# Attention scores as fp32 products on halves of TensorE's rows, with an eight-block weight ring and block products from the fifth chunk on

## The chip, the cores and the metric

The kernel runs on one core of one Trainium2 chip. The metric is the time of the whole kernel in device microseconds; the profiles give the span of one execution and what each engine did in it.

## The reference

Four batches of eight heads, 768 positions, 64 values a head. Each position sees the first `n_sink` = 4 keys and the last `window` = 128; its output goes through a feed-forward block with 512 inputs and 2048 inner values.

```python
scores = scale * np.matmul(q, k.transpose(0, 1, 3, 2))
...
keep = is_sink | in_window
scores = np.where(keep, scores, -1000000000.0)
scores = scores - np.max(scores, axis=-1, keepdims=True)
a = np.exp(scores)
a = a / (np.sum(a, axis=-1, keepdims=True) + 1e-09)
return np.matmul(a, v).astype(np.float32)
...
h = x @ w_in
g = h - np.tanh(h)
return (g @ w_out).astype(np.float32)
```

## The kernel before

**Chunks and units.** The 3072 rows are cut into 12 chunks of 256 rows (two query tiles of 128), numbered `cc` = 0 to 11: the first chunk of batches 0 to 2, then the other two of each of these, then the three of batch 3. A chunk's attention is four units `u`, each a pair of heads. Keys are laid out so that a query tile's keys (four sink keys and 256 positions) are 260 columns in a row; in the first tile of a batch only the last 132 of them are read by what follows.

**Attention of a unit** (`scores`, `normalise`, `turn`, `attend`). For each query tile and each head a product of queries and keys goes to a bank of its own in PSUM; VectorE merges and masks (`merge`), ScalarE takes the exponent, sums are inverted, TensorE transposes (L599), VectorE, ScalarE and GpSimd mask the transposed blocks, and TensorE multiplies with the values (L662). There the two heads of a pair have 64 output rows each and use the lower and upper 64 columns of the array.

**Two ways of scores.** For the first 12 units (`raw(u)`) queries and keys are multiplied as they are, in fp32 (L507). The 64 rows of the other head are zeros in the queries (cleared by GpSimd, L353, loaded in halves by `_load_pair`), so each product uses all 128 rows. The profile records such an fp32 product as two passes. For the later 36 units `split` makes high and low parts: ScalarE rounds keys and queries (L473, L483), VectorE subtracts (L478, L486), and four products of one pass each (L514) make the scores of a tile of two heads.

**Feed-forward.** A step `n` is one chunk with one of eight groups `g` of inner values. Its first half (`mm1`, L793) is 24 products of 256 columns. Its second half is 12 products of 512 columns (`mm2`, L863) or, from chunk `SA` = 5 on, 21 products of 256 columns that make the same result by blocks (`mm7`, L897). The block products need three sums of weight blocks for each group, the edge blocks: `derive` copies and adds them by DMA (L992, L995) and splits them. From chunk 3 on the first half's weights come from memory through a ring of seven blocks (`stream`; tiles `ring` and `spare`).

**Order.** Everything is added to a list with an engine, a price and a due time; `Work.order` puts it in order with these prices, and the engines run it in that order. The prices and due times are the constants `FIRST`, `PACE`, `LEAD` and others. Loads of the later units go through GpSimd's queue, the others through SyncE's.

Of the kernel before, what the change touches and what calls it, by code (L numbers as in the profile page):

```python
# [18 lines left out]
P = 128  # L19
# [21 lines left out]
def kernel(  # L41
# [20 lines left out]
    for m in range(2):  # L62
        first = pts[:, m].rearrange("p h a b -> p (h a b)")
        early.append((first[:, :KW], first[:, KW : KW + 2 * CH].rearrange("p (h s) -> p h s", h=2)))
    et = mybir.EngineType
    with tc.manual_schedule(engines={et.PE, et.SP, et.DVE, et.Activation, et.Pool}):
# [3 lines left out]
        for m in range(2):  # L70
            k, q = early[m]
            nc.sync.dma_start(k, kp[0, m, :, :KW])
            _load_pair(nc, q, qd[0, 2 * m : 2 * m + 2, :, :CH], True)
# [23 lines left out]
def _load_pair(nc, q, src, zeros):  # L97


    for h in range(2):  # L100
        r, z = slice(64 * h, 64 * h + 64), slice(64 * (1 - h), 64 * (1 - h) + 64)
        if zeros:
            nc.gpsimd.memset(q[z, h, :], 0.0)
        nc.sync.dma_start(q[r, h, :], src[h, r])
# [128 lines left out]
def _banded(tc, qd, kp, vp, vs, masks, w_in, w_out, ident, pts, early, out):  # L233
    nc = tc.nc
    et = mybir.EngineType
    with ExitStack() as ctx:
# [5 lines left out]
        qpool, kpool, vpool, hpool = pool("qpool", 1), pool("kpool", 1), pool("vpool", 3), pool("hpool", 1)  # L242
# [19 lines left out]
        SLK, PAD, LATE, LAND, QP, KP, BP, LEAD3 = 0.0, 1.05, 65222.0, 4372.0, 0, 0, 1, 89032.0  # L262
        SA, NSLOT, RING, GP, LQ, ST = 5, 7, 7, 0, 1, 1
# [9 lines left out]
        FIRST, EARLY, PACE, LEAD = 45000.0, 4600.0, 8242.0, 72963.0  # L273
        UNIT, SECOND, WLEAD, WNEXT = 2000.0, 3000.0, 6000.0, 2500.0
        HALF2, LAST = 8269.0, 4401.0
        SPILL, STREAM, DEAR, DLATE = 54590.0, 4000.0, 39769.0, 31275.0
# [38 lines left out]
        def slots(u):  # L315
            i = u if u < 4 or u in lent else 2
            return [("kt", i), ("qt", i)]

        def load_qk(u):
            cc, p, b, c = unit(u)  # L320

            def lend():
                if u == 3:
                    if u not in place_of:
                        place_of[u] = gpool.tile([P, 3 * WG // 2], F32, tag="spare", name="qk3")
                    return place_of[u]
# [5 lines left out]
            def keys():  # L332
                if u in lent or u == 3:
# [3 lines left out]
                (nc.gpsimd if LQ and not raw(u) else nc.sync).dma_start(kt[u], kp[b, p, :, 2 * c * TS : 2 * c * TS + KW])  # L337

            def queries():
                if not raw(u):  # L340
                    qt[u] = qpool.tile([P, 2, CH], F32, tag="qraw", name=f"qraw{u}")
                src = qd[b, 2 * p : 2 * p + 2, :, c * CH : (c + 1) * CH]
                if raw(u):
                    _load_pair(nc, qt[u], src, False)
                else:
                    (nc.gpsimd if LQ else nc.sync).dma_start(qt[u], src.rearrange("h d s -> d h s"))  # L346

            def zeros():
                if u in lent or u == 3:
                    qt[u] = lend()[:, : 2 * CH].rearrange("p (h s) -> p h s", h=2)  # L350
                else:
                    qt[u] = qpool.tile([P, 2, CH], F32, tag="qraw", name=f"qraw{u}")
                nc.gpsimd.memset(qt[u], 0.0)  # L353

            t = due_unit(u) - 8000
            if raw(u):
                work.add("POOL", 460, t - ZL, zeros, (), [slots(u)[1]])
            e = "POOL" if LQ and not raw(u) else "SP"
            work.add(e, 600, t, keys, (), [slots(u)[0], "seq k"], lands=800 if raw(u) else 1000)
            work.add(e, 800, t, queries, (), [slots(u)[1], "seq q"], lands=600 if raw(u) else 1000)  # L360
# [101 lines left out]
        qh, ql, ks, pr, st, xps, xh, xl, sps, tps = ({} for _ in range(10))  # L462

        def split(u):

            def k_high(h):
                if h == 0:
                    t = hpool.tile([P, NPAIR * CH], F32R, tag="ha", name=f"ks{u}")  # L470
                    ks[u] = t[:, : 2 * KW].rearrange("p (h k) -> p h k", h=2)
                r = slice(64 * h, 64 * h + 64)
                nc.scalar.copy(ks[u][r, h, :], kt[u][r, :])  # L473

            def k_low(h):
                k, t = ks[u], kt[u]
                r, o = slice(64 * h, 64 * h + 64), slice(64 * (1 - h), 64 * (1 - h) + 64)
                (nc.gpsimd if KP else nc.vector).tensor_tensor(k[o, h, :], t[r, :], k[r, h, :].bitcast(F32), op=ALU.subtract)  # L478

            def q_high():  # L480
                t = hpool.tile([P, 2, 2, CH], F32R, tag="hb", name=f"q{u}")
                qh[u], ql[u] = t[:, 0], t[:, 1]
                nc.scalar.copy(qh[u], qt[u])  # L483

            def q_low():
                (nc.gpsimd if QP else nc.vector).tensor_tensor(ql[u], qt[u], qh[u].bitcast(F32), op=ALU.subtract)  # L486

            t = due_unit(u) - 5000
            k, q = ([s] for s in slots(u))
            old = [("x", 2)] + [("xu", 2, i) for i in range(NPAIR)] if u == 3 * NPAIR else []  # L490
# [858 lines left out]
```

## Time and profile before

| what | value |
|---|---|
| median of 3 runs | 685.65 us (685.11 to 689.05) |
| profiled execution | 685.92 us, of it the span 684.2 us |
| TensorE busy | 665.0 us, 97% |
| VectorE, ScalarE, GpSimd busy | 78%, 60%, 30% |
| granted TensorE clock | 0.997 of 2.4 GHz |

The span runs from the first to the last instruction of the profiled execution. Products on TensorE overlap in the records, each shown with its run through the array, so the time that one costs is seen in the distance between starts.

### The profile page before, as it was taken

To read this page: it belongs to the slowest core of one execution; us is meant where nothing else is said; L and a number is where in the kernel's file an instruction comes from. 1 tells how busy PE (TensorE), PEld (TensorE's weight loads), DVE (VectorE), ACT (ScalarE), POOL (GpSimd) and SP (SyncE) were. 2 spreads that over 40 slices of the span, in tenths; PEclk is the share of its full clock that TensorE was granted. 3 is DMA by queue.
4 is the path that set the end of the run, shared out by engine and by line. 5 is a ranking of instruction groups with operands and counts; after the bars stand their busy time and mean duration, and the time that the engine had idled before them with its cause. 6 is when DMAs were issued, how large, how long until landed. Compare 5 with 4: busy or idle time off the path is not lost.

```text
span 684.2 us, 14570 instructions
## 1 busy us (share of the span) xinstructions
PE 665.0 (97%) x5099; PEld 613.8 (90%) x5099; DVE 531.4 (78%) x1365; ACT 412.7 (60%) x1056; POOL 204.7 (30%) x363
## 2 busy tenths in 40 slices
PE   6899999999999999999999999999999999999995
PEld 4677899989888898899999999999999999999995
DVE  6999988965998875577698797888888888755654
ACT  5986444435998876466676576676676567533331
POOL 5444000002985532334432323422223222300100
PEclk9999999999999999999999999999999999999998
DMA  6878896785999577799977767766667766656861
GB/s 178 269 252 273 283 308 242 285 280 155 199 209 289 182 228 222 216 290 284 265 223 215 230 176 233 231 209 207 215 216 231 245 192 168 206 160 196 261 187 35
DMA packets 79342, 152.96 MB, mean 224 GB/s; under 512 B 9565, under 2 KB 25565, under 8 KB 79261
## 3 DMA queue, kind: packets, MB, share of 16 engines
q1 hardware_dynamic: 65884, 121.65, 56.7%
q0 software_dynamic: 13376, 30.30, 16.4%
q8 instruction: 42, 0.69, 0.4%
q14 instruction: 40, 0.32, 0.1%
HBM read 131.47 MB, written 20.45 MB: 222 GB/s over the span
## 4 chain that ended last, share of the span: by engine, by line
PE 83%; POOL 4%; DVE 4%; ACT 4%; DMA 2%; issue 2%; SPq 0%; POOLq 0%; DVEq 0%; ACTq 0%
PE h L793 35%; PE s L897 11%; PE o L897 8%; PE o L863 8%; PE x L662 3%; PE s L863 3%; PE t L599 2%; PE t L662 2%; PE t L514 2%; PE t L863 2%; PE x L514 2%; PE x L863 2%; POOL edge L995 1%; PE s L514 1%; DMA v<-vp 1%
## 5 line engine op out<-in xcount | busy, mean ns | idle before, releaser
L793 PE MATMUL h<-xh,ring 128*128 128x256 f32 x660 | 133.5, 282 | 0.0
L812 ACT ACTIVATE gbuf<-h 128x512 f32<-128x512 f32 x96 | 57.2, 596 | 86.7 <-PE h L793 58.9
L793 PEld LDWEIGHTS h<-xh,ring 128*128 128x128 f32 x660 | 107.8, 188 | 0.4 <-PE t L662 0.2
L793 PE MATMUL h<-xh,spare 128*128 128x256 f32 x492 | 100.0, 283 | 0.0
L346 POOL DMA_DIRECT2D qraw<-qd x36 | 29.6, 821 | 222.7 <-DVE q L486 198.4
L793 PE MATMUL h<-xl,ring 128*128 128x256 f32 x330 | 92.2, 279 | 0.0
L539 ACT ACTIVATE p<-p,st 128x132 f32<-128x132 f32 x168 | 66.9, 400 | 27.8 <-DVE st L531 26.6
L831 ACT CAST ghbuf<-gbuf 128x896 fp32r<-128x896 f32 x55 | 51.8, 942 | 49.0 <-DVE gbuf L828 48.6
L793 PEld LDWEIGHTS h<-xh,spare 128*128 128x128 f32 x492 | 81.0, 190 | 0.3
L834 DVE TENSOR_TENSOR glbuf<-gbuf,ghbuf 128x896 fp32r<-128x896 f32 x55 | 60.3, 1097 | 20.1 <-ACT ghbuf L831 15.1
L793 PE MATMUL h<-xh,w 128*128 128x256 f32 x384 | 74.0, 282 | 0.0
L793 PE MATMUL h<-xl,spare 128*128 128x256 f32 x246 | 69.4, 282 | 0.0
L793 PEld LDWEIGHTS h<-xl,ring 128*128 128x128 f32 x330 | 62.1, 188 | 0.3
L793 PEld LDWEIGHTS h<-xh,w 128*128 128x128 f32 x384 | 61.1, 188 | 1.3 <-PE x L662 0.2
L565 ACT ACTIVATE p<-p,st 128x132 f32<-128x132 f32 x168 | 54.2, 394 | 3.5 <-DVE st L560 3.1
L815 DVE TENSOR_TENSOR gbuf<-h,gbuf 128x512 f32<-128x512 f32 x55 | 37.8, 687 | 21.9 <-ACT gbuf L812 21.3
L793 PE MATMUL h<-xl,w 128*128 128x256 f32 x192 | 53.8, 280 | 0.0
L619 POOL TENSOR_TENSOR pt<-pt,after 128x512 f32<-128x512 f32 x32 | 44.1, 1379 | 25.5 <-ACT pt L616 24.1
L863 PE MATMUL o<-w,ghbuf 128*128 128x512 f32 x192 | 50.8, 399 | 0.1
L793 PEld LDWEIGHTS h<-xl,spare 128*128 128x128 f32 x246 | 46.7, 190 | 0.3
L815 DVE TENSOR_TENSOR h<-h,gbuf 128x512 f32<-128x512 f32 x41 | 28.5, 695 | 19.1 <-ACT gbuf L812 19.0
L478 DVE TENSOR_TENSOR ks<-kraw,ks 64x392 fp32r<-64x392 f32 x72 | 40.5, 562 | 3.5 <-ACT ks L473 1.4
(174 smaller groups left out, 1693.2 us busy)
## 6 DMA issues: line engine op xcount, KB each, us to landing
ring<-wscr SPq DMA_DIRECT2D x165, 256.0 KB, 4.3
spare<-wscr SPq DMA_DIRECT2D x123, 256.0 KB, 4.5
qraw<-qd POOLq DMA_DIRECT2D x36, 256.0 KB, 5.2
wraw<-w_in SPq DMA_DIRECT2D x16, 512.0 KB, 6.4
wraw<-w_out SPq DMA_DIRECT2D x16, 512.0 KB, 6.9
wscr<-w SPq DMA_DIRECT2D x16, 512.0 KB, 6.0
kraw<-kp POOLq DMA_DIRECT2D x36, 196.0 KB, 4.5
v<-vp POOLq DMA_DIRECT2D x18, 256.0 KB, 3.3
```

What stands on the lines that cost most here:

```text
L478: (nc.gpsimd if KP else nc.vector).tensor_tensor(k[o, h, :], t[r, :], k[r, h, :].bitcast(F32), op=ALU.subtract)
L514: nc.tensor.matmul(ps[h][:, :WIN], lhsT=q[:, h, t * P : (t + 1) * P], rhs=rhs, start=i == 0, stop=i == 1,)
L539: nc.scalar.activation(e, e, AF.Exp, bias=st[u][:, j : j + 1], scale=-1.0, accum_out=st[u][:, 4 + j : 5 + j],)
L565: nc.scalar.activation(pr[u][:, j, :], pr[u][:, j, :], AF.Copy, scale=s[:, 8 + j : 9 + j])
L619: nc.gpsimd.tensor_tensor(w[:, :, 0, :], w[:, :, 0, :], after.unsqueeze(1).to_broadcast([P, 4, P]), op=ALU.mult)
L793: nc.tensor.matmul(hps[n][:, f, :], lhsT=w, rhs=x, start=r == 0, stop=r == 11)
L812: nc.scalar.activation(g0, h(), AF.Tanh)
L815: nc.vector.tensor_tensor(g0 if strassen(n) else h(), h(), g0, op=ALU.subtract)
L831: nc.scalar.copy(ghbuf[:, n % 2], gbuf[:, 1:, :])
L834: nc.vector.tensor_tensor(glbuf[:, :7, :], gbuf[:, 1:, :], ghbuf[:, n % 2].bitcast(F32), op=ALU.subtract)
L863: nc.tensor.matmul(sums_of(n, cc, t), lhsT=a[:, f, t * P : (t + 1) * P], rhs=wt[1, g][:, (0, 1, 0)[i], f, :], start=first and not low and ...
L897: nc.tensor.matmul(acc, lhsT=a[:, b, :], rhs=factor(g, m, part % 2), start=g == 0 and part == 0 and m in (4, 1, 2, 7), stop=closes(n) and ...
```

## The change

All 48 units now use fp32 scores. Queries and keys of the two heads of a unit lie in the upper and the lower 64 partitions, without zeros, and each head's product reads its 64 rows only: one uses rows 0 to 63 of the array, the other rows 64 to 127, each with a bank of its own as before. `split` is gone, with its tiles; in the first tile of a batch only the 132 columns that are read are multiplied. Later units are loaded two ahead into two buffers. The space of the splits holds four blocks of the ring, which has eight now. `SA` is 4, so the fifth chunk (`cc` = 4) uses block products and leaves the plain second half. The planner's price of a tile's scores becomes 470 ns, or 250 for 132 columns (890 and 490 before), and its due times are set anew.

```diff
-def _load_pair(nc, q, src, zeros):
...
+def _pair(qd, b, p):
...
+    return qd[b, 2 * p : 2 * p + 2].rearrange("h r s -> (h r) s")[D : 3 * D]
...
-        qpool, kpool, vpool, hpool = pool("qpool", 1), pool("kpool", 1), pool("vpool", 3), pool("hpool", 1)
+        qpool, kpool, vpool, hpool = pool("qpool", 2), pool("kpool", 2), pool("vpool", 3), pool("hpool", 1)
...
-        SA, NSLOT, RING, GP, LQ, ST = 5, 7, 7, 0, 1, 1
+        SA, NSLOT, RING, GP, LQ, ST = 4, 7, 8, 0, 1, 1
...
-        FIRST, EARLY, PACE, LEAD = 45000.0, 4600.0, 8242.0, 72963.0
...
+        FIRST, EARLY, PACE, LEAD = 34738.0, 4600.0, 8156.0, 62753.0
...
-        def split(u):
...
-                    if raw(u):
-                        nc.tensor.matmul(
-                            ps[h][:, :WIN], lhsT=qt[u][:, h, t * P : (t + 1) * P],
-                            rhs=kt[u][:, t * TS : t * TS + WIN], start=True, stop=True,
-                        )
-                        continue
-                    rhs = ks[u][:, h, t * TS : t * TS + WIN]
-                    for i, q in enumerate((qh[u], ql[u])):
-                        nc.tensor.matmul(
-                            ps[h][:, :WIN], lhsT=q[:, h, t * P : (t + 1) * P], rhs=rhs,
-                            start=i == 0, stop=i == 1,
-                        )
+                    r, a = slice(D * h, D * h + D), 0 if kind else P
+                    nc.tensor.matmul(
+                        ps[h][:, a:WIN], lhsT=qt[u][r, t * P : (t + 1) * P],
+                        rhs=kt[u][r, t * TS + a : t * TS + WIN], start=True, stop=True,
+                    )
...
-                ring["b"] = gpool.tile([P, 3, WG // 2], F32R, tag="spare", name="spare")
-            ring[i] = ring["b"][:, i - 4, :] if i > 3 else ring["a"][:, i, :]
+                ring["b"] = [hpool.tile([P, 2, WG // 2], F32R, tag=t, name="ring") for t in ("ha", "hb")]
+            ring[i] = ring["b"][(i - 4) // 2][:, i % 2, :] if i > 3 else ring["a"][:, i, :]
...
-                if RAW <= u + 1 < NU:
-                    load_qk(u + 1)
+                if RAW <= u + 2 < NU:
+                    load_qk(u + 2)
...
-                if cc == SA - 1:
+                if n - 1 == last_plain(g):
                     derive(g, 6)
```

TensorE's order at the start, before (`s` and `o` are the score banks, `pt`, `qraw`, `kraw` and `qk` loaded queries and keys, `t` transposed probabilities):

```order
L507 MATMUL s_236<-kraw_261,qraw_259 128x260
L507 MATMUL s_237<-kraw_261,qraw_259 128x260
L507 MATMUL o_238<-kraw_261,qraw_259 128x260
L507 MATMUL o_239<-kraw_261,qraw_259 128x260
L599 MATMUL t<-ident,p_273 128x128 x4
L507 MATMUL s_236<-qk_277 128x260
L507 MATMUL s_237<-qk_277 128x260
```

There the third unit's two tiles, the first transposes and the fourth unit's first tile follow each other. TensorE's order at the same place now:

```order
L458 MATMUL s_230<-kraw_257,qraw_267 128x132
L458 MATMUL s_231<-kraw_257,qraw_267 128x132
L458 MATMUL o_232<-kraw_257,qraw_267 128x260
L458 MATMUL o_233<-kraw_257,qraw_267 128x260
L458 MATMUL s_230<-kraw_297,qraw_299 128x132
L458 MATMUL s_231<-kraw_297,qraw_299 128x132
```

The first tile of each unit has 132 columns in place of 260, and the fourth unit's scores stand ahead of the first transposes. The first 12 units' scores stand in 10 unbroken groups.

TensorE's order in the fourth chunk's attention, among feed-forward products (L793 first half, L863 second half), before:

```order
L793 MATMUL h_1999<-xh_473,w_5_1394 128x256
L514 MATMUL s_236<-ks_1988,q_1981 128x260 x2
L514 MATMUL s_237<-ks_1988,q_1981 128x260 x2
L599 MATMUL t<-ident,p_1936 128x128 x4
L793 MATMUL h_1999<-xh_473,w_5_1394 128x256
```

There one tile's scores of two heads are four split products. TensorE's order in the fourth chunk's attention now (L734 is the first half, L804 the second):

```order
L734 MATMUL h_1821<-xh_462,w_4_1292 128x256
L458 MATMUL s_230<-kraw_646,qraw_715 128x260
L458 MATMUL s_231<-kraw_646,qraw_715 128x260
L734 MATMUL h_1821<-xh_462,w_4_1292 128x256
L734 MATMUL h_1821<-xl_463,w_4_1292 128x256
```

Two fp32 products on half the rows stand where four split ones stood, again alone between products on the whole array; so do all 72 groups of the later units.

TensorE's order in the fifth chunk's first step, its second half, before:

```order
L863 MATMUL o_239<-w_0_781,ghbuf 128x512 x4
L863 MATMUL o_238<-w_0_781,glbuf 128x512 x2
L863 MATMUL o_239<-w_0_781,glbuf 128x512 x2
L793 MATMUL h_3317<-xh_2838,spare 128x256
L793 MATMUL h_3317<-xl_2839,spare 128x256
```

These are the last 8 of its 12 products of 512 columns and the next first half. TensorE's order in that half now:

```order
L838 MATMUL s_230<-edge_1760,ghbuf 128x256 x4
L838 MATMUL o_233<-edge_1760,ghbuf 128x256 x2
L838 MATMUL s_231<-w_0_828,ghbuf 128x256 x4
L838 MATMUL o_232<-w_0_828,ghbuf 128x256 x4
L838 MATMUL s_230<-edge_1760,glbuf 128x256 x2
L838 MATMUL o_233<-edge_1760,glbuf 128x256
L838 MATMUL s_231<-w_0_828,glbuf 128x256 x2
L838 MATMUL o_232<-w_0_828,glbuf 128x256 x2
```

The 21 block products that stood in the sixth chunk's first step stand in the fifth chunk's now.

## Rows read from the trace of the kernel before

**Rows 1.** The page: busy time of each engine; the chain that ended last.

```profile
PE 665.0 (97%) x5099; PEld 613.8 (90%) x5099; DVE 531.4 (78%) x1365; ACT 412.7 (60%) x1056; POOL 204.7 (30%) x363
...
PE 83%; POOL 4%; DVE 4%; ACT 4%; DMA 2%; issue 2%; SPq 0%; POOLq 0%; DVEq 0%; ACTq 0%
```

**Rows 2.** Stretch, length, busy us (count) of PE, PEld, DVE, ACT, POOL; clock, DMA.

```profile
10.00:20.00 10.00, 6.87 (x35) 5.04 (x34) 7.69 (x44) 8.27 (x35) 2.83 (x11) 1.00 0.82 253
20.00:30.00 10.00, 9.19 (x64) 6.44 (x62) 8.90 (x39) 9.39 (x40) 4.12 (x10) 1.00 0.90 280
30.00:42.00 12.00, 10.24 (x62) 7.27 (x60) 11.14 (x43) 10.23 (x37) 6.38 (x15) 1.00 0.81 250
42.00:60.00 18.00, 17.59 (x130) 14.67 (x128) 16.13 (x53) 15.55 (x53) 8.55 (x17) 1.00 0.81 271
60.00:80.00 20.00, 19.19 (x125) 16.19 (x124) 19.28 (x25) 8.68 (x15) 2.99 (x3) 1.00 0.86 292
...
200.00:320.00 120.00, 119.65 (x854) 107.01 (x851) 86.13 (x248) 83.62 (x231) 51.35 (x85) 1.00 0.81 240
320.00:600.00 280.00, 279.59 (x2408) 269.80 (x2407) 233.16 (x623) 182.62 (x453) 84.74 (x147) 1.00 0.71 217
```

**Rows 3.** Waits of all engines: total us, times, longest us.

```profile
DVE p L531 <- PE o L507: 2.1, 1, 2.1
```

**Rows 4.** Order of time on PE, first units: start us, length us, instructions.

```profile
25.42 1.04 PE L507 MATMUL s<-qk 128*128 128x260 f32 x4
26.30 0.60 PE L599 MATMUL t<-ident,wide 128*128 128x128 f32 x4
26.74 0.38 PE L640 MATMUL x<-ident,z 128*128 128x128 f32 x2
```

**Rows 5.** Order of time on PE, chunk 3's scores.

```profile
162.86 0.64 PE L514 MATMUL s<-ks,q 128*128 128x260 f32 x4
163.33 0.29 PE L793 MATMUL h<-xh,w 128*128 128x256 f32 x1
```

**Rows 6.** Order of time on PE, a plain and a block second half.

```profile
63.93 2.03 PE L863 MATMUL s<-w,ghbuf 128*128 128x512 f32 x8
65.80 1.10 PE L863 MATMUL s<-w,glbuf 128*128 128x512 f32 x4
...
618.32 0.63 PE L897 MATMUL s<-edge,ghbuf 128*128 128x256 f32 x4
...
620.80 0.28 PE L793 MATMUL h<-xh,ring 128*128 128x256 f32 x1
```

**Rows 7.** Order of time on PE around the values of a later chunk.

```profile
438.03 0.40 PE L656 MATMUL x<-zr,vsink 128*128 128x512 f32 x1
438.26 0.40 PE L656 MATMUL t<-zr,vsink 128*128 128x512 f32 x1
438.59 1.96 PE L662 MATMUL x<-pt,v 128*64 128x256 f32 x24
440.38 1.91 PE L662 MATMUL t<-pt,v 128*64 128x256 f32 x24
442.21 0.50 PE L897 MATMUL s<-edge,glbuf 128*128 128x256 f32 x2
442.56 0.28 PE L897 MATMUL o<-edge,glbuf 128*128 128x256 f32 x1
```

**Rows 8.** Groups of VectorE: xcount, busy us, mean ns, idle before, releaser.

```profile
L478 DVE TENSOR_TENSOR ks<-kraw,ks 64x392 fp32r<-64x392 f32 x72 | 40.5, 562 | 3.5 <-ACT ks L473 1.4
...
L486 DVE TENSOR_TENSOR q<-qraw,q 128x512 fp32r<-128x512 f32 x36 | 25.8, 717 | 4.4 <-ACT q L483 4.4
```

**Rows 9.** Waits of all engines, weight loads (PEld).

```profile
PEld x L662 <- issue: 4.1, 13, 0.4
```

**Rows 10.** Instructions of L995 and L897: ns min/median/max, first and last start us.

```profile
L995 POOL DMA_DIRECT2D edge<-bscr x24: 863/1184/2175, 161.3 to 205.3; - x24
...
L897 PE MATMUL s<-edge,ghbuf x220: 277/281/386, 327.7 to 672.0; 128*128 128x256 f32 x110
```

More of the change, by code (lines that the diff above doesn't have):

```diff
@@ L63 @@
         first = pts[:, m].rearrange("p h a b -> p (h a b)")
-        early.append((first[:, :KW], first[:, KW : KW + 2 * CH].rearrange("p (h s) -> p h s", h=2)))
+        early.append((first[:, :KW], first[:, KW : KW + CH]))
     et = mybir.EngineType
@@ L315, in slots @@
         def slots(u):
-            i = u if u < 4 or u in lent else 2
+            i = u if u < 2 or u in lent else u % 2 + 2
             return [("kt", i), ("qt", i)]
@@ L336, in keys @@
                     kt[u] = kpool.tile([P, KW], F32, tag="kraw", name=f"kraw{u}")
[L337 removed]
+                a = 0 if c else P
+                (nc.gpsimd if LQ and not raw(u) else nc.sync).dma_start(
+                    kt[u][:, a:], kp[b, p, :, 2 * c * TS + a : 2 * c * TS + KW]
+                )
             def queries():
[L340 to L353 removed]
+                if u in lent:
+                    qt[u] = lend()[:, :CH]
+                else:
+                    qt[u] = qpool.tile([P, CH], F32, tag="qraw", name=f"qraw{u}")
+                (nc.gpsimd if LQ and not raw(u) else nc.sync).dma_start(qt[u], _pair(qd, b, p)[:, c * CH : (c + 1) * CH])
             t = due_unit(u) - 8000
[L356 to L357 removed]
             e = "POOL" if LQ and not raw(u) else "SP"
[L359 to L360 removed]
+            work.add(e, 600, t, keys, (), [slots(u)[0], "seq k"], lands=800 if c else 550)
+            work.add(e, 600, t, queries, (), [slots(u)[1], "seq q"], lands=500)
         vslot, vnew = {}, []
@@ L459, in sink_values @@
             work.add("DVE", 500, due - 1000, total, [slot], ["vsink"], port=True)
-        qh, ql, ks, pr, st, xps, xh, xl, sps, tps = ({} for _ in range(10))
-        def split(u):
[L468 to L490, printed above, removed]
-            work.add("ACT", 525, t, q_high, q, ["qh"] + old)
-            work.add("POOL" if QP else "DVE", 1360 if QP else 705, t, q_low, q + ["qh"], ["ql"], port=True)
-            for h in range(2):
-                work.add("ACT", 425, t, lambda h=h: k_high(h), k, [("ks", h)] + old)
-                work.add("POOL" if KP else "DVE", 1050 if KP else 590, t, lambda h=h: k_low(h), k, [("ks", h)], port=True)
+        pr, st, xps, xh, xl, sps, tps = ({} for _ in range(7))
         def scores(u, t):
@@ L545, in scores @@
             s = ["o0", "o1"] if apart else ["s0", "s1"] if cc <= SA else ["t", "x"]
-            if raw(u):
-                src, took = slots(u), 890
-            else:
-                src, took = ["qh", "ql", ("ks", 0), ("ks", 1)], 490
+            src, took = slots(u), 470 if kind else 250
             work.add("PE", took, d, products, src, s)
@@ L980, in _banded, with last_plain @@
         ends_with = []
+        def last_plain(g):
+            return max(n for n, (cc, x) in enumerate(order) if cc < SA and x == g)
         def derive(g, m):
@@ L1005, in rest_of @@
                     nc.vector.tensor_tensor(lo, lo.bitcast(F32), hi, op=ALU.subtract)
-            d = due_step(order.index((SA, g))) - DEAR if m != 6 else due_step(order.index((SA - 1, g))) + DLATE
+            d = due_step(order.index((SA, g))) - DEAR if m != 6 else due_step(last_plain(g)) + DLATE
             w = [("w", 1, g)] if m == 6 else [("e", g, m)]
@@ L1034, in store, with old @@
             nc.sync.dma_start(out[r0 : r0 + P, :], ob[cc, t])
+        def old(n):
+            if order[n] == (3, 0):
+                return [("w", 0, 1)]
+            if order[n] == (3, 1):
+                return [("x", 2)] + [("xu", 2, i) for i in range(NPAIR)]
+            return []
         def first_half(n):
@@ L1040, in first_half @@
                     work.add("SP", 500, due_step(n) - STREAM + 700 * j, lambda j=j: stream(n, j),
-                             [("scr", g, j // 2)], [("ring", ring_at(n, j))] + ([("w", 0, 1)] if cc == 3 and g == 0 else []), lands=850)
+                             [("scr", g, j // 2)], [("ring", ring_at(n, j))] + old(n), lands=850)
             for f in range(2):
@@ L1088, in attention @@
             for u in range(NPAIR * cc, NPAIR * cc + NPAIR):
-                if not raw(u):
-                    split(u)
                 for t in range(2):
```

25 lines of the change are left out of this document (8 added, 17 removed).

## The prediction

> **What bounds the kernel now.** I read the page's busy times and its chain of waits first, then busy times by stretch, then the order of time on TensorE (PE) at the places that the change touches. TensorE is busy in 97% of the span and holds 83% of the chain that ended last [rows 1]; between 320 and 600 us it is idle for 0.4 us of 280 [rows 2]. So a TensorE nanosecond saved after about 80 us comes off the end, and one added goes onto it, while time saved on VectorE (DVE) or ScalarE (ACT) gives nothing unless TensorE waited for it. The start is different: up to 42 us TensorE has idle time, and there VectorE is the fuller engine; from 60 to 80 us both are full [rows 2].
>
> The profiled execution took 685.92 us, 1.72 us more than its span of 684.2; the median of the runs is 685.65. My sums are made against 685.9.
>
> A busy row of TensorE overlaps its neighbour, so I price a product by the distance from its start to the start of what follows. A raw pair (two heads, each product recorded as two passes over 260 columns) takes 25.42 to 26.30, 0.88 us, for 4 records: 0.22 each [rows 4]. The four split products of a later tile take 162.86 to 163.33, 0.47 us [rows 5].
>
> **The change part by part.**
>
> *Scores of the later 36 pairs of heads (72 groups, one per pair and query tile).* Four split products leave, two raw products of 64 rows come, one in the upper and one in the lower half of the array. The trace of before has no product on half the rows. Bounds: the two run side by side and cost 0.88/2 = 0.44 us, or one after the other and cost 0.88. The nearest row for side by side is the product of probabilities and values (L662), whose two heads lie in the two halves of the array's columns: 24 records, 8 of 256 and 16 of 128 columns, would take 8 x 0.216 + 16 x 0.108 = 3.46 us in a row at the raw pace of 0.22 per 260 columns; they took 1.79 and 1.83 us [rows 7]. So halves do run together, and I take 0.44. Four of the 72 (first tile of the last batch) read 132 columns instead of 260: 0.22. Sum: 72 x 0.47 = 33.8 becomes 68 x 0.44 + 4 x 0.22 = 30.8: **-3.0 us**. By the Trainium skill's "TensorEngine Tiling (Array Packing)", section "Key Properties", tiles operate independently; the column halves agree with it (1.79 us against 3.46), and no run here shows the rows.
>
> *What it costs to go into such a group and out again.* This is where I choose. For column halves there is a price, in [rows 7]: the product before them takes 0.33 us where its equal takes 0.23 (+0.10), the 48 records take 3.62 us where twice half of 3.46 would do (+0.16), and the two products after them take 0.35 where two take 0.24 at the pace of [rows 6], 2.48/21 each (+0.11): 0.37 us a group. The waits say the same: the weight load of L662 stood 13 times for 0.3 us for nothing that the profile shows [rows 9]. For a change of kind on the whole array there is none: 0.47 us between the starts at 162.86 and 163.33 is 4 x 0.118, the pace of products of nearly the same width [rows 5, 6], so no time is lost around it, and the transposes behind a raw pair start on its pace [rows 4]. Ends: 0 and 0.37 us a group. The column halves are the nearer row in that the array is divided; the whole-array rows are nearer in that row halves keep all 128 columns, a whole bank as output and one moving stream of 128 partitions, and it is another splitting of columns, weights and stream that sets the column halves apart. I take 0 and give the other end its own case below.
>
> *Scores of the first 12 pairs (24 groups).* 0.88 becomes 0.22 for the 12 tiles of 132 columns and 0.44 for the other 12: 24 x 0.88 = 21.1 becomes 7.9, -13.2 us on TensorE. Not all of it reaches the end, because VectorE has the same merges, masks and weight decoding as before. Its idle time from 10 to 80 us is 2.3 + 1.1 + 0.9 + 1.9 + 0.7 = 6.9 us [rows 2], and its first wait for scores, 2.1 us [rows 3], can shrink by some 1.5. So at most 8.4 us, which I take: **-8.4**; ends -2 (VectorE's idle time stays, since ScalarE and the DMAs make it) and -13.2 (VectorE catches up after 80 us). If weight loads of two halves do not run together, a group of 132 columns has four loads; four transposes, whose 128 columns are as narrow, follow each other at 0.11 us [rows 4], so such a group would cost 0.44, not 0.22: 16 x 0.22 = +3.5 us. I take 0 and keep 3.5 for the range.
>
> *Loads.* Ten clearings on GpSimd (POOL) and one of three loads per early pair go; keys of a batch's first chunk come without the 128 columns that nothing reads, queries of the later pairs in half the bytes. Both queues get shorter, and later pairs are asked for two ahead in two buffers instead of one ahead in one. Cost 0: it is SyncE's (SP's) and GpSimd's time, and GpSimd is 30% busy [rows 1].
>
> *Splits.* VectorE loses 36 x 717 ns and 72 x 562 ns, 66 us [rows 8], ScalarE the matching casts. TensorE had little from waiting for them: its idle time from 200 to 600 us is 0.35 + 0.41 = 0.76 us [rows 2]. I count all of it: **-0.8 us**. The raw products need only the loaded keys and queries; what is late next is the merge on VectorE that frees the score banks, and it is unchanged.
>
> *Fifth chunk by block products.* A step's second half was 12 products of 512 columns; eight take 63.93 to 65.80, so 12 take 2.81 us. As 21 products of 256 columns it takes 618.32 to 620.80, 2.48 us [rows 6]. Eight steps x 0.33 = **-2.6 us**. The price is 24 edge blocks that must be ready eight steps earlier; in the kernel before they are added up between 161 and 205 us and first used at 327.7 [rows 10]. Eight steps are 8 x (24 x 0.118 + 2.81) = 45 us of products and some 10 of attention between them, so the first use moves to about 272 us, and I count no wait. From here on scores of the sixth chunk share their banks with the transposes, as all later chunks do already: 0.
>
> *Ring of eight blocks.* TensorE never waited for a ring block: its idle time is too small for it [rows 2]. 0.
>
> Sum: -3.0 - 8.4 - 0.8 - 2.6 = -14.8; 685.9 - 14.8 = 671.1, and as much below the median: **671 us**.
>
> **The rivals.**
>
> *Switching costs (slower).* If each group on row halves pays what a group on column halves pays, the 72 later groups each stand alone between products of the whole array, as the order shows, and pay 72 x 0.37 = 26.6 us on TensorE at full length; the first 24 form 10 groups, 3.7 us, half of which I count: 671.1 + 26.6 + 1.9 = **700 us**. Weight loads of 128 columns instead of 64 in the open would add up to 0.1 us a group, 707. It decides from 14.8/72 = 0.21 us a group on. For it: [rows 7, 9]. Against it: the whole-array rows. The Trainium skill, "TensorEngine Tiling (Array Packing)", "Key Properties", speaks for it: a change of tiling mode, not just of tile, drains the engine. By that rule the sum is this rival's 700; the column halves agree with it by their 0.37 us, and no row shows row halves.
>
> *The halves run one after the other (the change does not do what it says).* Then a later group costs 0.88: 68 x 0.41 = +27.9, less 0.1 for the four narrow ones; the early pairs save only by their width, 12 x 0.44 = 5.3, of which 3.4 counts in the forecast's proportion; 685.9 + 27.8 - 3.4 - 2.6 - 0.8 = **707 us**. Against it: [rows 7].
>
> *The start gives nothing.* Halves run together and switch freely, but VectorE's idle time stays (-2) and narrow groups are bound by their loads (+3.5): 671.1 + 6.4 + 3.5 = **681 us**, no measurable change. For it: VectorE at 8.9 of 10 and 11.1 of 12 us [rows 2].
>
> **How the numbers follow.** Chances: forecast 0.55 (its own range 665 to 679, from about all 13.2 us of the start's gain to little of it), nothing from the start, or a switch of up to 0.2 us, 0.13; switching costs 0.23; one after the other 0.06; slower by something else 0.03. Under 1% a measurement of this kernel can hardly tell from no change, that is 678.8 to 692.5. Faster by over 1%: 0.56, the forecast and a little of the third rival; same: 0.13; slower: 0.31. The range must take in most of the switching case to leave out no more than 2 in 10: 665 to 705.
>
> **What would show it.** In the profile after, the two heads' score records should start together, and the distance from the first of them to the next whole-array product should be about 0.44 us (0.22 for 132 columns); 0.8 us, with weight loads that wait for nothing shown, is the switching rival; four starts 0.22 apart are the serial one. TensorE's products of the first feed-forward steps should come some 4 to 8 us earlier than in the kernel before; if they do not, the start gave nothing. From the fifth chunk on a second half should take 2.5 us and TensorE should not be idle in front of an edge block. The forecast is wrong above all if the array's division by rows must be set up as the one by columns is.

## The result and the profile after

The changed kernel takes 695.1 us (median of 4 runs, 694.07 to 698.28) where the kernel before took 685.58 (4 runs, 685.11 to 689.05): a ratio of 1.0135, 95% interval 1.0115 to 1.0156. The forecast was 671; the time is slower by 1.35% and near the rival "switching costs", which gave 700.

First the page of the changed kernel: busy time of each engine, and the chain that ended last by engine.

```profile
PE 675.1 (97%) x5171; PEld 595.9 (86%) x5171; DVE 489.1 (71%) x1287; ACT 364.7 (53%) x947; POOL 182.6 (26%) x351
...
PE 91%; ACT 2%; DVE 2%; DMA 2%; SPq 1%; POOL 1%; issue 1%; DVEq 0%; POOLq 0%; ACTq 0%
```

Against [rows 1], VectorE lost 42 us and ScalarE 48 us of busy time, as the splits left and more block sums came. TensorE's share of the last chain rose from 83% to 91%: it is more alone on the path than before, so time that it loses is lost at the end.

Busy time by stretch, to be held against [rows 2]: length, busy us (count) of PE, PEld, DVE, ACT, POOL, then the granted clock and DMA.

```profile
20.00:30.00 10.00, 8.36 (x56) 5.42 (x58) 8.91 (x38) 8.93 (x38) 1.66 (x9) 0.83 0.75 255
30.00:42.00 12.00, 10.60 (x59) 6.75 (x57) 10.06 (x43) 10.62 (x40) 5.37 (x15) 0.72 0.67 208
320.00:600.00 280.00, 279.52 (x2342) 255.32 (x2341) 198.78 (x547) 146.61 (x373) 72.27 (x142) 1.00 0.65 198
```

And in pieces of 2 us, ahead of the first fall of the clock and in it:

```profile
18.00:20.00 2.00, 1.52 (x12) 0.95 (x12) 1.90 (x6) 2.00 (x8) 1.52 (x3) 1.00 0.14 48
20.00:22.00 2.00, 1.08 (x5) 0.92 (x5) 1.92 (x11) 2.00 (x11) 1.04 (x6) 0.76 0.12 33
22.00:24.00 2.00, 2.00 (x11) 1.20 (x12) 1.97 (x6) 1.84 (x9) 0.00 (x0) 0.50 0.89 255
```

Two things stand out. The granted clock, 1.00 before, is 0.83 and 0.72 in the two stretches at the start, and goes down to 0.50 in them. And from 320 to 600 us TensorE is as full as before (279.52 us of 280), but did 2342 products where it had done 2408. It is not idle: its products, or the places between them, take longer.

Where that time lies is seen in the order of time on TensorE around one score group: start us, length us, and the products in a row.

```profile
401.16 0.40 PE L838 MATMUL s<-edge,glbuf 128*128 128x256 f32 x2
401.39 0.28 PE L838 MATMUL o<-edge,glbuf 128*128 128x256 f32 x1
401.60 0.48 PE L458 MATMUL t<-kraw,qraw 64*128 64x260 f32 x1
401.61 0.48 PE L458 MATMUL x<-kraw,qraw 64*128 64x260 f32 x1
401.93 0.38 PE L458 MATMUL t<-kraw,qraw 64*128 64x260 f32 x1
401.93 0.38 PE L458 MATMUL x<-kraw,qraw 64*128 64x260 f32 x1
402.24 0.50 PE L838 MATMUL s<-w,glbuf 128*128 128x256 f32 x2
402.58 0.40 PE L838 MATMUL o<-w,glbuf 128*128 128x256 f32 x2
402.82 0.28 PE L734 MATMUL h<-xh,ring 128*128 128x256 f32 x1
```

The two heads (banks `t` and `x`) start 0.01 us apart, pass by pass: the halves do run together. But the block product ahead of them, alone, takes 0.21 (401.39 to 401.60) where a product in a row takes 0.12; the passes take 0.32 and 0.31 where a full-speed pass takes 0.22; and the two block products behind them take 0.34 (402.24 to 402.58) where the next two take 0.24. That is 0.09 + 0.10 + 0.09 + 0.10. In all, the group holds the engine from 401.51 (0.12 behind 401.39) to 402.34 (0.24 ahead of 402.58), 0.83 to 0.84 us, where the four split products held it for 0.47 [rows 5]. The place is no exception: over the 68 groups of 260 columns the two passes take 0.64 us together in the median, and a first-half product ahead of a group, as 29 of them have, takes 0.21.

The waits of weight loads in the changed kernel (total us, times, longest) show the same places:

```profile
PEld h L734 <- issue: 9.3, 30, 0.3
PEld o L804 <- issue: 5.9, 18, 0.3
PEld s L838 <- issue: 4.1, 13, 0.3
PEld o L838 <- issue: 3.9, 12, 0.3
```

Before, only the values, whose heads lie in column halves, had such a row of size [rows 9]. Now the loads of the feed-forward products (L734, L804, L838), which stand behind the score groups, have waited 73 times for 0.3 us for nothing that the profile shows; there are 72 score groups behind the start.

Last, what the start gave: the first and last starts of the early first-half products (ns min, median, max; us).

```profile
L734 PE MATMUL h<-xh,w x384: 276/279/392, 42.4 to 191.3; 128*128 128x256 f32 x192
```

The first product of the feed-forward block comes at 42.4 us, as it did before (41.9). That is no sum of the start, for some of the first 12 units' attention stands behind it. At the first product of step 6 (144 products of 24 to a step stand ahead of it) all of that attention is done in both kernels and no later group has come. Its start, now and before, and then TensorE's busy time, with the count, of second halves (L804, before L863) up to there:

```profile
82.40 0.28 PE L734 MATMUL h<-xh,w 128*128 128x256 f32 x1
```

```profile
86.79 0.28 PE L793 MATMUL h<-xh,w 128*128 128x256 f32 x1
```

```profile
0.00:82.40 82.40, 13.57 (x48) 8.01 (x48) 0.94 0.75 248
```

```profile
0.00:86.79 86.79, 15.59 (x60) 10.62 (x60) 1.00 0.78 250
```

The step starts 4.4 us earlier, but 12 products of 0.23 us [rows 6], 2.8 us, are still to be done. So the start gave 1.6 us. The first later group stands at 162.9 us in both kernels, and everything else happened behind step 6.

### The profile page after: what moved, and what is told of

Read it like the earlier page. It is cut to its first block, busy times and chain, and to the rows that moved or that the text cites. A ratio compares the mean times of both kernels' runs of the same rounds, so it can differ in the third digit from the quotient of the medians.

```text
span 693.2 us, 14463 instructions
## 1 busy us (share of the span) xinstructions
PE 675.1 (97%) x5171; PEld 595.9 (86%) x5171; DVE 489.1 (71%) x1287; ACT 364.7 (53%) x947; POOL 182.6 (26%) x351
## 4 chain that ended last, share of the span: by engine, by line
PE 91%; ACT 2%; DVE 2%; DMA 2%; SPq 1%; POOL 1%; issue 1%; DVEq 0%; POOLq 0%; ACTq 0%
PE h L734 39%; PE s L838 13%; PE o L838 10%; PE o L804 7%; PE t L458 5%; PE x L603 4%; PE s L804 3%; PE t L540 3%; PE t L603 2%; PE t L804 2%; PE x L804 2%; PE s L458 1%; DMA qraw<-qd 1%; DMA wraw<-w_out 1%; DVE pt L554 1%
## 5 line engine op out<-in xcount | busy, mean ns | idle before, releaser
L734 PE MATMUL h<-xh,ring 128*128 128x256 f32 x1152 | 221.9, 283 | 0.0
L734 PEld LDWEIGHTS h<-xh,ring 128*128 128x128 f32 x1152 | 182.3, 188 | 8.7 <-issue 7.6
L734 PE MATMUL h<-xl,ring 128*128 128x256 f32 x576 | 160.9, 279 | 0.0
L734 PEld LDWEIGHTS h<-xl,ring 128*128 128x128 f32 x576 | 108.3, 188 | 0.4
L734 PE MATMUL h<-xh,w 128*128 128x256 f32 x384 | 75.4, 282 | 0.0
L734 PEld LDWEIGHTS h<-xh,w 128*128 128x128 f32 x384 | 61.5, 188 | 3.6 <-issue 1.7
L734 PE MATMUL h<-xl,w 128*128 128x256 f32 x192 | 53.5, 279 | 0.0
L939 POOL DMA_DIRECT2D edge<-bscr x24 | 23.4, 1324 | 96.7 <-DMA edge<-bscr 96.4
L554 DVE TENSOR_TENSOR pt<-t,below 128x512 f32<-128x512 f32 (+1 forms) x48 | 28.8, 600 | 21.7 <-PE t L540 12.7
L838 PE MATMUL s<-edge,ghbuf 128*128 128x256 f32 x252 | 42.4, 287 | 0.0
L838 PE MATMUL o<-w,ghbuf 128*128 128x256 f32 x252 | 41.8, 284 | 0.0
L838 PE MATMUL s<-w,ghbuf 128*128 128x256 f32 x252 | 40.7, 280 | 0.0
L458 PE MATMUL t<-kraw,qraw 64*128 64x260 f32 (+1 forms) x112 | 38.5, 423 | 0.7 <-ACT pt L557 0.7
```

Of the source, the lines that this page charges most:

```text
L458: nc.tensor.matmul(ps[h][:, a:WIN], lhsT=qt[u][r, t * P : (t + 1) * P], rhs=kt[u][r, t * TS + a : t * TS + WIN], start=True, stop=True,)
L734: nc.tensor.matmul(hps[n][:, f, :], lhsT=w, rhs=x, start=r == 0, stop=r == 11)
L838: nc.tensor.matmul(acc, lhsT=a[:, b, :], rhs=factor(g, m, part % 2), start=g == 0 and part == 0 and m in (4, 1, 2, 7), stop=closes(n) and ...
```

## The experiments

The theory after the result: going into a score group on half the rows and out of it costs some 0.4 us. The rivals: products on half the rows are slow in themselves; the time is lost to the other order of work or to one of the other parts. Each kernel ran in 4 runs or more; the kernel before had medians of 685.6 to 686.3 beside them, so a difference of a microsecond between two kernels with 4 runs each says little.

**Twice the work in each group** (`twice`).

```diff
-                for h in range(2):
+                for h in [0, 1] * (1 if raw(u) else 2):
```

> The changed kernel, but each of the 72 later score groups does its two products twice over, one time right behind the other, so that there is twice the work on halves of the rows and as many changes to it and back. If the price lies in going into a group and out of it (0.38 us of the 0.83 that a group takes), a group grows by one pair, 0.45 us, and the four narrow ones by 0.22: 68 x 0.45 + 4 x 0.22 = +31 us on 695.1, 727 us, and the trace shows the pair in the middle at its bare pace. If the products on half the rows are themselves slow, a group doubles: 72 x 0.83 = +59, about 754 us.

It took 724.4 us (ratio 1.056, 1.0543 to 1.0578), 29.3 more than the changed kernel. One of its groups, in order of time on TensorE:

```profile
399.16 0.28 PE L734 MATMUL h<-xh,ring 128*128 128x256 f32 x1
399.37 0.48 PE L458 MATMUL t<-kraw,qraw 64*128 64x260 f32 x1
...
399.69 0.38 PE L458 MATMUL t<-kraw,qraw 64*128 64x260 f32 x1
...
399.91 0.38 PE L458 MATMUL t<-kraw,qraw 64*128 64x260 f32 x1
...
400.13 0.38 PE L458 MATMUL t<-kraw,qraw 64*128 64x260 f32 x1
...
400.45 0.73 PE L838 MATMUL s<-edge,ghbuf 128*128 128x256 f32 x4
```

The passes in the middle start 0.22 apart, the full pace; only the first and the last take 0.32. The price is in the edges of a group, not in its products.

**The later groups on the whole array** (`full_late`), two products one after the other, nothing divided. This one came last, to settle the size.

```diff
-                    r, a = slice(D * h, D * h + D), 0 if kind else P
+                    r, a = slice(D * h, D * h + D) if raw(u) else slice(0, P), 0 if kind else P
```

> The changed kernel, but each of the 72 later score groups multiplies on all 128 rows, two products of two passes over 260 columns one after the other; the separation of the pair's two heads is left out there, so each head's scores are the sum of both heads'. Order and loads stay. A group then takes 0.88 us with no change of the array's division around it, the four narrow ones 0.44. If a group on half the rows takes 0.84 us with its way in and out, as the distances between starts say, this costs 68 x 0.04 = +3 us: 698 us. If the way in and out costs only the 0.27 us that taking it away gave (19.4 us over 72), a group takes 0.71 now, and this costs 68 x 0.17 = +12: 707 us.

It took 698.29 us (1.018, 1.0148 to 1.0212), 3.2 more than the changed kernel: the first case. One of its groups:

```profile
403.27 0.28 PE L838 MATMUL o<-edge,glbuf 128*128 128x256 f32 x1
403.39 0.60 PE L458 MATMUL t<-kraw,qraw 128*128 128x260 f32 x2
403.83 0.60 PE L458 MATMUL x<-kraw,qraw 128*128 128x260 f32 x2
404.07 0.59 PE L838 MATMUL s<-w,glbuf 128*128 128x256 f32 x2
404.50 0.39 PE L838 MATMUL o<-w,glbuf 128*128 128x256 f32 x2
```

The product ahead takes its 0.12, so nothing is lost going in; four passes of 0.22 and the next two products end at 404.50, 0.24 ahead of which the group ends: 403.39 to 404.26, 0.87 us. Twice the passes on the whole array cost nearly what half of them cost on halves of it. So it is not fp32 scores between other products that cost 0.40 us, but their lying on half the rows.

**One product of the whole array in each group** (`one_full`), 0.44 us, what the forecast gave a pair on halves.

```diff
-                for h in range(2):
-                    r, a = slice(D * h, D * h + D), 0 if kind else P
+                for h in range(2 if raw(u) else 1):
+                    r, a = slice(D * h, D * h + D) if raw(u) else slice(0, P), 0 if kind else P
```

> The changed kernel, but each of the 72 later score groups is a single product on all 128 rows (two passes over 260 columns, 0.44 us, the time that the forecast gave a pair on half the rows); it leaves the second head's product out, and its bank keeps old sums. The order on every engine stays that of the changed kernel. If going into and out of a group on half the rows costs 0.38 us and nothing else of the change is slow, 72 x 0.38 = 27.4 us come off 695.1: 668 us, near the forecast's 671. If the changed kernel is slower for another reason (its order of work, the block products of the fifth chunk, its ring), the time stays above 685 us.

It took 675.71 us (0.9861, 0.9828 to 0.9894): 19.4 less than the changed kernel, 8.0 short of the 27.4. Some of that shows as new waits of TensorE (total us, times, longest):

```profile
PE s L458 <- DMA qraw<-qd: 3.2, 2, 1.9
PE s L458 <- DVE st L475: 2.2, 2, 1.5
PE t L540 <- ACT p L506: 1.9, 3, 1.4
```

In the changed kernel the first two were 0.7 and 1.2, and the third wasn't there. With the switching gone, TensorE runs into loads, merges and normalisation. So 19.4 is what the switching was worth at the end of this plan, and 0.4 us a group what it costs on the engine; `full_late`, which doesn't let TensorE run ahead, fits the second.

**The splits left out of the kernel before** (`nosplit`). The later units' products use unit 12's parts, and `split` is added for that unit alone.

```diff
-                if not raw(u):
+                if u == RAW:
                     split(u)
...
-                    rhs = ks[u][:, h, t * TS : t * TS + WIN]
-                    for i, q in enumerate((qh[u], ql[u])):
+                    rhs = ks[RAW][:, h, t * TS : t * TS + WIN]
+                    for i, q in enumerate((qh[RAW], ql[RAW])):
```

> The kernel before, but only the first of the 36 later pairs of heads is split into its parts, and the later pairs' products use those parts again; it leaves out the splitting of 35 pairs, and TensorE's products are the same in number and shape. If the splits cost TensorE waits that the idle time does not show, as the distances between starts before and after suggest, 10 to 13 us come off: 673 to 676 us. If they cost only the idle time that the views show, 0.8 us comes off: 685 us, which cannot be told from no change.

It took 710.11 us (1.0351, 1.0315 to 1.0386): 24 slower with less to do, which neither case had. Without the splits in the list, `Work.order` puts the rest in another order, and TensorE meets waits that it hadn't; the largest:

```profile
PE x L640 <- POOL z L576: 5.4, 2, 4.0
```

So the run says nothing on the splits, and much on the plan. **With the plan held** (`nosplit_same`), the splits stay in the list with their prices, and for the later units issue nothing:

```diff
             def k_high(h):
+                if u > RAW:
+                    return
```

(and so in `k_low`, `q_high` and `q_low`; the products as in `nosplit`).

> The kernel before with the splits of 35 of the 36 later pairs left out (their products use the first pair's parts again), this time with the places of the splits kept in the plan, so that all other work stands in the order of the kernel before on every engine. TensorE's products are the same in number, shape and order. If TensorE lost 10 to 13 us to the splits in waits too short to be seen as idle time, the time falls to 673 to 676 us. If it lost only the visible 0.8 us, it is 685 us, and the 707 to 712 of the replanned version came from its other order.

It took 685.15 us (0.9986, 0.9976 to 0.9995), 1.0 less than the kernel before: the second case. The splits hid no 10 us; my theory of hidden waits fell here. The 25 us between the two kernels are the order alone.

**The fifth chunk**, from both sides: block products from the fifth chunk on in the kernel before (`sa4`), and only from the sixth on in the changed one (`after_sa5`).

```diff
-        SA, NSLOT, RING, GP, LQ, ST = 5, 7, 7, 0, 1, 1
+        SA, NSLOT, RING, GP, LQ, ST = 4, 7, 7, 0, 1, 1
```

> The kernel before, with block products from the fifth chunk on and nothing else of the change. If the edge blocks are ready in time, the eight second halves give 8 x 0.33 = 2.6 us: 683.0 us. If TensorE has to wait for edge blocks that are needed eight steps earlier, or the sixth chunk's scores wait for the banks that they now share with the transposes, nothing is left of it or it is slower: 685 to 690 us.

> The changed kernel with block products from the sixth chunk on, as in the kernel before. If the fifth chunk by block products is worth the predicted 8 x 0.33 us, the time rises by 2.6 us to 697.7. If it is worth nothing or costs something here, it stays at 695 or falls.

`after_sa5` took 697.64 us, 2.5 more than the changed kernel: the eight halves are worth about what was predicted. `sa4` took 699.38 (1.0203, 1.0182 to 1.0225), 13.1 slower than its kernel before. Its fifth chunk did gain (its step 40 starts at 314.4 us, before at 317.3), and then its TensorE stood still. Its two long waits, in order of time on TensorE, and three stretches show it:

```profile
338.35 0.46 PE L793 MATMUL h<-xh,spare 128*128 128x256 f32 x1 [3.71 <-issue]
...
395.77 0.36 PE L793 MATMUL h<-xh,ring 128*128 128x256 f32 x1 [2.33 <-issue]
```

```profile
330.00:340.00 10.00, 6.15 (x44) 5.72 (x43) 8.67 (x16) 4.34 (x11) 4.71 (x8) 0.92 0.69 205
340.00:350.00 10.00, 10.00 (x93) 8.35 (x93) 6.24 (x13) 3.92 (x9) 2.92 (x6) 0.91 0.37 117
...
390.00:400.00 10.00, 7.67 (x53) 6.23 (x53) 8.13 (x11) 2.95 (x5) 3.30 (x5) 0.83 0.67 220
```

TensorE is idle for 3.71 and 2.33 us in front of products that read ring blocks, and the granted clock is lower in the stretches of the two holes and just behind the first (0.92, 0.91; 0.83). **The ring** in the changed kernel cut to seven blocks (`ring7`, the third constant of that line) was to tell whether it is its length:

> The changed kernel with a ring of seven blocks instead of eight. By the prediction's step the ring is worth nothing: 695 us. By what the kernel before showed with block products from the fifth chunk on and a ring of seven (feed-forward products waiting 3.7 and 2.3 us for a ring block between 330 and 400 us, and the stretches at a lower clock behind them), a ring of seven is too short once block products begin earlier: 700 to 708 us.

It took 695.59 us (1.0141, 1.012 to 1.0161): no change, as the prediction had it. So seven blocks are enough in the changed kernel's plan. In `sa4`'s, where the loads are asked for otherwise, they seem to come too late: the profile shows nothing that the two products waited for, and the loads are inferred from what they read. Which entry of the plan does it, and whether an eighth block would have helped there, was not tried.

**The first 12 units on the whole array** (`full_early`, the same edit as `full_late` with the cases of `raw(u)` exchanged) and **extra work that keeps TensorE going at the start** (`fill`).

> The changed kernel, but the scores of the first 12 pairs are multiplied on all 128 rows; the separation of the pair's two heads is left out there, so each head's scores are the sum of both heads' (same widths, 132 and 260 columns; a group takes 0.44 or 0.88 us instead of 0.22 or 0.44, and none has a change of the array's division around it). If the gain on TensorE at the start was eaten by the changes of division and by the stretches at the lower clock, the granted clock stays at 1.00 from 20 to 42 us, the first product of the feed-forward step comes at 41.5 to 42.5 us as in both kernels, and the time stays at 693 to 697 us. If the half-array products did give time back at the start that was then lost later, the first feed-forward product comes 4 to 8 us later and the time is 699 to 703 us.

`full_early` took 693.52 us (1.0107, 1.0089 to 1.0124), 1.6 less than with halves; the two intervals overlap a little. Its stretches at the start:

```profile
20.00:30.00 10.00, 7.35 (x57) 5.10 (x57) 9.44 (x39) 9.74 (x41) 1.91 (x9) 1.00 0.75 239
30.00:42.00 12.00, 10.38 (x69) 7.40 (x66) 10.23 (x48) 10.83 (x41) 5.32 (x15) 1.00 0.70 214
```

The clock stays at 1.00 and the first feed-forward product comes at 41.2 us. With twice the passes, TensorE was no later: ScalarE (9.74 and 10.83 us) and VectorE fill these stretches.

```diff
+        dummy = []
...
+            def fill():
+                if not dummy:
+                    dummy.append(ps_h.tile([P, 2, CH], F32, tag="h", name="dummy"))
+                for _ in range(3):
+                    nc.tensor.matmul(dummy[0][:, 0, :P], lhsT=ident, rhs=ident, start=True, stop=True)
+
+            if apart and u < 8:
+                work.add("PE", 660, d + 100, fill, ["o0"], ["dummy"])
```

> The changed kernel with three products of 128 columns on all 128 rows, which nobody reads, behind the score products of each of the first eight pairs, 8 x 0.66 = 5.3 us of TensorE's time. If the granted clock fell at the start because of what TensorE did there, it stays at 1.00 from 20 to 42 us; if the fallen clock held the start back, the first feed-forward product then comes 1 to 3 us earlier (40 to 41.5 us) and the time falls to 692 to 694. If the start waits for other engines, the time stays at 695, and if TensorE's own time counts there, it rises to 697 to 700.

`fill` took 695.16 us (1.0146, 1.0108 to 1.0185). In its profiled execution the clock was 1.00 from 20 to 30 us and 0.86 from 30 to 42, and the first feed-forward product came at 41.1 us; the median didn't move. But neither run shows what made the clock fall. In the profiled execution of `ring7`, whose scores at the start lie on halves too, it stayed at 1.00:

```profile
20.00:30.00 10.00, 9.28 (x67) 5.93 (x68) 9.46 (x39) 9.67 (x40) 2.28 (x10) 1.00 0.72 243
30.00:42.00 12.00, 10.27 (x76) 6.93 (x73) 10.93 (x48) 11.74 (x45) 5.39 (x15) 1.00 0.71 216
```

And in that of `nosplit`, whose scores lie on the whole array, it was 0.86 from 20 to 30 us. In `ring7` the first feed-forward product came at 40.2 us and step 6 at 80.77, 2.2 and 1.6 us ahead of the changed kernel, with the same 456 products in the same order on TensorE up to step 6. If the clock is all that differs, it took some 2 us from the start of the changed kernel in that one execution; at the end the two differ by 0.13 us (694.85 and 694.98). The extra work costs next to nothing: the start waits for other engines.

**The place of the buffers.** Comparing the two traces product by product, I found one difference that no part of the change speaks of: block products and first halves follow each other faster after. The order of time on TensorE in the changed kernel, the second halves of two steps that follow each other:

```profile
623.12 0.64 PE L838 MATMUL s<-edge,ghbuf 128*128 128x256 f32 x4
...
625.60 0.28 PE L734 MATMUL h<-xh,ring 128*128 128x256 f32 x1
...
628.45 0.63 PE L838 MATMUL s<-edge,ghbuf 128*128 128x256 f32 x4
...
630.84 0.28 PE L734 MATMUL h<-xh,ring 128*128 128x256 f32 x1
```

21 products take 2.48 us in the one, as before [rows 6], and 2.39 in the other. The change had made the loaded keys and queries other sizes, and so had moved every activation buffer behind them. Three kernels move them by a few bytes of padding (`before_pad32`, `before_pad64` with 16 words for 8, `after_pad32`); all three also clear the padding once on GpSimd:

```diff
+        pad = hpool.tile([P, 8], F32, tag="pad", name="pad")
         pp, sm = pool("pp", 2), pool("sm", 4)
...
+        nc.gpsimd.memset(pad, 0.0)
```

> The kernel before, with 32 bytes of padding in SBUF ahead of the buffers of activations (xh, xl, gbuf, ghbuf, glbuf and those between them), which moves them from addresses that are 32 past a multiple of 64 to multiples of 64, as they lie in the changed kernel; the instructions and their order stay. In the trace of the kernel before a block product follows the last by 118.4 ns on average, in that of the changed one by 114.5, and a product of a first half by some 1 ns more before than after. If the place of these buffers makes that difference, 1155 block products x 3.9 ns = 4.5 us and about 2300 x 1 ns = 2.3 us come off: 679 us. If the change's other traffic made it, nothing happens: 686 us.

> The same with 64 bytes of padding, so that the buffers move but stay 32 past a multiple of 64. If the multiple of 64 decides, nothing happens: 686 us. If any move of the buffers changes the pace, it differs from 686.

> The changed kernel with 32 bytes of padding at the same place, which puts the same buffers 32 past a multiple of 64, as in the kernel before. If their place makes the pace, 1323 block products x 3.9 ns = 5.2 us and some 2.2 us in the first halves are added: 702 us, and the block products follow each other by 118 ns. If not, 695 us.

| kernel | us | ratio to before, interval | what was expected |
|---|---|---|---|
| `before_pad32` | 683.13 | 0.9956, 0.9937 to 0.9975 | 679 |
| `before_pad64` | 688.35 | 1.0028, 1.0012 to 1.0045 | 686 |
| `after_pad32` | 702.36 | 1.0223, 1.0182 to 1.0264 | 702 |

The stretch from 320 to 600 us, in this order:

```profile
320.00:600.00 280.00, 279.34 (x2428) 269.62 (x2427) 234.33 (x621) 182.48 (x451) 84.17 (x147) 1.00 0.71 217
```

```profile
320.00:600.00 280.00, 279.59 (x2395) 270.50 (x2396) 233.19 (x621) 181.76 (x452) 84.14 (x147) 1.00 0.72 218
```

```profile
320.00:600.00 280.00, 279.54 (x2310) 255.74 (x2309) 195.96 (x544) 145.17 (x371) 71.17 (x141) 1.00 0.64 196
```

TensorE is equally full in all, and the count of products goes from 2408 [rows 2] to 2428 and 2395, and from 2342 to 2310. In the changed kernel the move of 32 bytes costs 7.3 us, as expected from the pace. In the kernel before it gives 2.7, less than half of the 6.8 expected, and 64 bytes cost 2.5 where nothing was expected; the two have the same clearing, so it is the move that makes the 5.2 us between them. So the place of the buffers changes the pace, but a multiple of 64 is not the whole rule; which buffers and which places count stays open.

**A faster version** (`pad_narrow`): the kernel before with that padding, and 132 columns instead of 260 where the first 128 are not read.

```diff
+                a = 0 if kind else P
                 for h in range(2):
                     if raw(u):
                         nc.tensor.matmul(
-                            ps[h][:, :WIN], lhsT=qt[u][:, h, t * P : (t + 1) * P],
-                            rhs=kt[u][:, t * TS : t * TS + WIN], start=True, stop=True,
+                            ps[h][:, a:WIN], lhsT=qt[u][:, h, t * P : (t + 1) * P],
+                            rhs=kt[u][:, t * TS + a : t * TS + WIN], start=True, stop=True,
```

> The kernel before with the 32 bytes of padding and, for the tiles at the start of a batch among the first 12 pairs, score products of 132 columns instead of 260 (the first 128 are never read); all 128 rows, nothing divided. TensorE is spared 12 x 0.44 = 5.3 us at the start. If the start waits for VectorE, ScalarE and the loads, as the first feed-forward product of the changed kernel says (42.4 us against 41.9), this gives 0 to 2 us on top of the padding: 677 to 679 us. If TensorE's time counts there, it gives 3 to 5: 674 to 676.

It took 682.04 us (0.9932, 0.9913 to 0.9951), the lowest time of a kernel that does all the work, and 1.1 below the padding alone, where the two intervals overlap: at the start TensorE's time, 5.3 us less here, counts for little.

## Why the prediction was wrong

**The step that failed** is "What it costs to go into such a group and out again", where I took 0 of the ends 0 and 0.37. It costs 0.40 on TensorE (0.84 less the 0.44 of the products), a little over the price of column halves [rows 7]. A later group was to go from 0.47 to 0.44 and took 0.84, which decided the sign. Over all 72 groups of the two profiled executions it is 21.5 us lost where -3.0 was forecast: 40.5 us before and 62.0 after, from a group's first product to the next other product, with what the products right ahead and right behind took above the median of their kind. Counted in the same way, `twice` has 29.4 us more than the changed kernel and `full_late` 2.7 more; their times rose by 29.3 and 3.2. I had the right row in hand and argued it away with whole-array rows, which show only that a change of product costs nothing while the array is undivided. Even that held for one place and not for all: before, 22 of the 72 groups took 0.51 to 1.04 us and not 0.47, so the 33.8 us of the sum was too low for what leaves. That the halves run together was right. The Trainium skill, "TensorEngine Tiling (Array Packing)", "Key Properties", says that a change of tiling mode, not just of tile, drains the engine; the runs agree with it, at 0.40 us in and out. How much of that is draining, and how much weight loads that nothing hides, no run here separates.

**Scores of the first 12 pairs**, -8.4: mis-sized. At step 6 the start had given 1.6 us, under the lower end of 2 that was given; `ring7`, at the full clock, had 3.2 by the same count. Halves themselves gave nothing there, since `full_early` was no slower without them. VectorE, ScalarE and the loads set the start; and it was ScalarE, not VectorE as I read it, that was the fuller of the two in the stretches from 10 to 30 us [rows 2].

**Splits**, -0.8: right, 1.0 with the plan held. **Fifth chunk**, -2.6: right, 2.5. **Ring**, 0: right, +0.5 without it, within the noise. **Loads**, 0: not tried by themselves.

**What no step had:** the buffers moved. With them 32 bytes further on the changed kernel takes 7.3 us more (`after_pad32`), so their new place seems to have given it about that much. It is one place against another: what the very places of the kernel before would cost in the changed kernel no run shows.

The sum with measured terms: +21.5 for the later groups, -1.6 for the start, -1.0, -2.5 and -7.3 give +9.1; measured were +9.5. That the two come so near is in part luck, as each of the smaller terms is known to a microsecond or so.

The rival "switching costs" had the mechanism and, at 0.37 a group, nearly the price. Its 700 was 5 too high through errors that ran against each other: the start gave 1.6 us and not 6.5, the groups lost 21.5 and not 23.6 (26.6 less 3.0), and the buffers gave 7.3 that it didn't know of.

## What to carry to other kernels

A group of products on a part of TensorE's array that stands alone between products of the whole array pays at both edges, here 0.40 us, nearly the 0.44 that its two products cost: divide the array where many such products stand in a row, or leave it whole (four passes on all rows cost 0.87 against 0.84). When one row of a trace shows a price for something near and another shows none for something farther, keep the price. In a kernel with a planned order, an experiment that takes work out must keep its place in the plan, or it measures the plan: here 710 against 685 us.

## What the hardware showed that I had not expected

- Moving the activation buffers by 32 bytes changed the time of the same products in the same order by 7.3 us in one kernel and 2.7, the other way, in another, with TensorE equally full.
- The granted clock at the start differs between executions of the same score products. In the changed kernel's it fell to 0.50 between 22 and 24 us, with TensorE busy for 1.52 and 1.08 us of the two pieces of 2 us ahead of that; in that of `ring7` it stayed at 1.00, with TensorE busy for 1.43 and 2.00 us of the same two pieces. What decides it stays open.
